# Real and imaginary rows packed in 96, logarithms summed in two parts, the sign from bits, and a new written-out order

## The chip, the cores and the metric

The kernel runs on one core of a Trainium2 chip. The metric is the device time of one execution in microseconds. Matrix products run on TensorE (PE in the profile, its weight loads PEld), elementwise work on VectorE (DVE) and ScalarE (ACT), a little on GpSimd (POOL); SyncE (SP) issues most DMAs.

## The reference

Two blocks follow each other. The first is a gated linear recurrence with a complex gate for each of 4 x 8 heads, 768 tokens and 48 channels; the second is a mixer over tokens of rank 32 and a two-layer network over 384 channels.

```python
mag = np.sqrt(a_re * a_re + a_im * a_im)
scale = np.minimum(mag, 0.999) / (mag + 1e-06)
a_re_n, a_im_n = (a_re * scale, a_im * scale)
for t in range(S):
    ar, ai = (a_re_n[:, :, t, :, None], a_im_n[:, :, t, :, None])
    new_re = ar * S_re - ai * S_im
    new_im = ar * S_im + ai * S_re
    kv = np.einsum('bhd,bhe->bhde', k[:, :, t], v[:, :, t])
    S_re, S_im = (new_re + kv, new_im)
    y[:, :, t] = np.einsum('bhd,bhde->bhe', q[:, :, t], S_re)
# x: the heads side by side, (4, 768, 384)
h = xt @ U @ V                      # xt: x with tokens last
u = x + h.transpose(0, 2, 1)
ch = np.maximum(u @ w_ch1, 0.0) @ w_ch2
out = u + ch
```

## The kernel before

Tokens are cut into 24 chunks of 128 (six for each of the four batches), two chunks to a group, so there are groups 0 to 11. The recurrence is not stepped: products of gates over a stretch of tokens are written as the exponential of a sum of logarithms of magnitudes and a turn by a sum of angles.

*Gates and totals* (`gates(g)`, rank "gates"): ScalarE and VectorE make from a_re and a_im the logarithm of the clipped magnitude, in two parts that stand in tiles `l` and `y` and are added on VectorE. TensorE sums the logarithm over tokens with constant matrices (`summed`: two sums for each chunk, line 696 for groups 0 to 2 in fp32, line 692 for the later groups, which split the logarithm in two fp32r tiles), and sums blocks of tokens (`of_blocks`: line 735 and line 741). ScalarE takes exponentials; the totals go by four DMAs into a tile T.

*Angles* (`turns_of`, `angles`, rank "angles"): an Arctan, a sign and a constant give the angle z (line 760), which is written over `y`; TensorE sums it over tokens; ScalarE takes sine and cosine into `cs`. The sign of a_re comes in groups 0 to 2 from its bits, by a VectorE operation that also puts 1/pi in (line 678), and in groups 3 to 11 from ScalarE's Sign; those groups then scale the angle and add a quarter in one more ScalarE operation. ScalarE works with two tables of functions in turn, so each group has two switches (line 381).

*Chunks* (`prep`, `chain`): q and k are multiplied by the exponentials and by sine and cosine into QKC, which holds for each head 48 real and 48 imaginary columns, each padded to 64. TensorE transposes QKC (line 860), from 64 tokens by 112 columns, to 112 partitions by 64 tokens, real rows at 0 and imaginary rows at 64. Products inside a chunk (lines 907, 910, 971), the state dk and its carrying on (line 996), and y (lines 1027, 1035) follow.

*Mixers* (`mixer(m)`): for each two chunks a product with w_ch1 (`up`, line 1122, or a scheme of fewer products, line 1222, in the last ones) and with w_ch2 (`down`, lines 1313 and 1356). The first mixer's six up-products are made before the mixing over tokens is known and are corrected later.

What runs when is written out by hand: each operation is added to a plan with its engine, a guessed cost and its rank, and ORDER gives, for each engine and rank, the place of each operation in one long list of 2671 places; each engine works through its operations in the order of their places. SPARE lists, for a place, how many blocks of 128 columns of idle matmul TensorE is given ahead of that operation. `idle` (line 1519) issues them, up to three blocks at a time, as a product of the identity with itself into a PSUM tile that is about to be used; where no such tile is free it issues nothing.

## Time and profile before

| | |
|---|---|
| three runs | 629.67, 630.09, 630.41 us; median 630.09 |
| profiled execution, span from the first to the last instruction | 627.0 us |
| its own time with what lies around the span | not given by itself; the median of the runs is 3.1 us above the span |
| TensorE busy, idle matmuls included | 609.9 us (97%) |
| VectorE busy | 499.7 us (80%) |
| ScalarE busy | 415.8 us (66%) |
| granted TensorE clock, mean | 0.995 |

A row of the groups names line, engine, operation, the tile written and those read, partitions by elements, and the count; then the busy time in us and the mean ns of one; then the engine's idle time just before, and what ended most of it. A row of the stretches gives the stretch and its length, the busy time and the number of instructions of PE, PEld, DVE, ACT and POOL (or of the engines chosen), then the granted clock, the share of DMA busy, and GB/s. A row of the waits gives who waited for whom, the sum, how often and the longest, in us. A row of the chain gives the start and the length of a piece in us.

### The profile page before, as it was taken

What the parts mean: (1) busy time and instruction counts of PE and PEld (TensorE: products, weight loads), DVE (VectorE), ACT (ScalarE), POOL (GpSimd) and SP (SyncE); (2) the same over time, 40 slices, a digit from 0 to 9 for tenths busy, and PEclk for the clock granted to TensorE, in tenths of its full rate; (3) what the DMA queues carried; (4) which work ended last, traced back from release to release, by engine and by line L of the source; (5) the groups of instructions that cost most, each with busy time, mean ns of one, the idle gap of its engine ahead of it and who ended that gap; (6) DMA issues with size and microseconds to landing.
All of it is one profiled execution on the core that took longest, in us unless ns stands there. A gap on an engine that the chain in (4) does not pass through costs nothing.

```text
span 627.0 us, 23447 instructions
## 1 busy us (share of the span) xinstructions
PE 609.9 (97%) x10380; PEld 526.2 (84%) x10380; DVE 499.7 (80%) x887; ACT 415.8 (66%) x807; POOL 38.1 (6%) x79
## 2 busy tenths in 40 slices
PE   6998989999999999999999999999999999999998
PEld 3566767666889889889989989888999998999997
DVE  6899999888999979758977867788989884464554
ACT  6999999999898988687787867688433431202010
POOL 5000000000001010010000100000100100000100
PEclk7999999999999999999999999999999999999999
DMA  8864565644143252541512512601203020000101
GB/s 211 191 146 115 135 136 132 155 111 104 33 80 76 50 120 44 99 89 28 99 37 46 113 40 46 124 19 25 63 21 60 9 51 3 1 1 1 45 14 44
DMA packets 173685, 45.74 MB, mean 73 GB/s; under 512 B 167632, under 2 KB 170384, under 8 KB 173584
## 3 DMA queue, kind: packets, MB, share of 16 engines
q1 hardware_dynamic: 171376, 39.90, 30.1%
q0 software_dynamic: 2208, 4.35, 2.1%
q8 instruction: 81, 1.33, 0.9%
q14 instruction: 20, 0.16, 0.1%
HBM read 33.59 MB, written 4.72 MB: 61 GB/s over the span
## 4 chain that ended last, share of the span: by engine, by line
PE 77%; ACT 4%; DVE 3%; DMA 1%; issue 1%; SPq 0%; ACTq 0%; DVEq 0%
PE down L1356 24%; PE up L1122 15%; PE few L1222 11%; PE dk L996 3%; PE tr L860 3%; PE y L1035 3%; PE inner L910 2%; PE down L1313 2%; PE inner L907 2%; PE tot L741 2%; PE y L1027 2%; PE mixed L1089 2%; PE es ps L692 1%; PE ef ps L692 1%; PE uTp L1107 1%; PE corners L971 1%
## 5 line engine op out<-in xcount | busy, mean ns | idle before, releaser
L1122 PE MATMUL up<-uT,w 128*128 128x256 f32 x504 | 116.9, 383 | 0.0
L387 DVE TENSOR_TENSOR QK<-QK,T 112x512 f32<-112x512 f32 (+2 forms) x144 | 102.1, 732 | 8.4 <-PE inner L910 4.3
L1122 PEld LDWEIGHTS up<-uT,w 128*128 128x128 f32 x504 | 93.6, 190 | 12.5
L1356 PE MATMUL down<-w,h 128*128 128x192 f32 x396 | 72.2, 331 | 0.0
L384 ACT ACTIVATE gate<-gate 128x768 f32<-128x768 f32 (+1 forms) x82 | 64.8, 795 | 7.4 <-DVE GS L791 3.2
L1356 PEld LDWEIGHTS down<-w,h 128*128 128x128 f32 x396 | 64.1, 190 | 1.5 <-issue 0.7
L871 ACT COPY QK<-tr 112x512 f32<-112x512 f32 x96 | 51.2, 590 | 14.6 <-PE tr L860 14.3
L390 DVE TENSOR_TENSOR xo<-down,xo 128x192 f32<-128x192 f32 (+1 forms) x79 | 29.9, 387 | 27.5 <-PE down L1356 27.0
L387 DVE TENSOR_TENSOR QKC<-qk,cs 128x768 f32<-128x768 f32 x44 | 41.7, 955 | 6.3 <-ACT cs L384 3.6
L1230 ACT COPY h<-few 128x512 f32<-128x512 f32 x30 | 17.2, 586 | 40.8 <-PE few L1222 40.8
L1356 PE MATMUL down<-stage 128*128 128x192 f32 x198 | 37.6, 331 | 0.0
L1111 ACT COPY uT<-uTp 128x384 f32<-128x384 f32 x22 | 10.0, 479 | 41.4 <-PE uTp L1107 26.9
L1222 PE MATMUL few<-gate,w 128*128 128x128 f32 x280 | 34.8, 275 | 0.0
L1298 POOL DMA_DIRECT2D out_dram<-xo x32 | 19.2, 644 | 243.3 <-DVE xo L390 140.0
L860 PEld LDWEIGHTS tr<-ident,QKC 64*112 64x112 f32 x768 | 24.5, 130 | 10.7 <-issue 4.7
L1222 PEld LDWEIGHTS few<-gate,w 128*128 128x128 f32 x280 | 33.3, 192 | 0.0
L1356 PEld LDWEIGHTS down<-stage 128*128 128x128 f32 x198 | 32.1, 190 | 0.7 <-issue 0.2
L779 POOL DMA_DIRECT2D gate<-F x15 | 12.0, 799 | 327.9 <-DVE w L578 113.5
L860 PE MATMUL tr<-ident,QKC 64*112 64x64 f32 x768 | 29.4, 221 | 2.3 <-DVE QKC L387 1.6
L381 ACT ACT_TABLE_LOAD x24 | 30.8, 1283 | 1.1 <-PEq L1573 0.7
L384 ACT ACTIVATE h<-up 128x512 f32<-128x512 f32 x42 | 24.6, 596 | 9.8 <-PE up L1122 9.5
L976 ACT COPY AT<-corners 32x128 f32<-32x128 f32 x96 | 24.2, 255 | 9.6 <-PE corners L971 8.3
(200 smaller groups left out, 1285.4 us busy)
## 6 DMA issues: line engine op xcount, KB each, us to landing
stage<-in_moe_w_ch_dram SPq DMA_DIRECT2D x12, 768.0 KB, 5.0
qk<-in_q_dram SPq DMA_DIRECT2D x24, 192.0 KB, 3.2
qk<-in_k_dram SPq DMA_DIRECT2D x24, 192.0 KB, 2.7
VP<-in_v_dram SPq DMA_DIRECT2D x24, 192.0 KB, 3.6
gate<-in_a_re_dram SPq DMA_DIRECT2D x22, 192.0 KB, 3.4
gate<-in_a_im_dram SPq DMA_DIRECT2D x22, 192.0 KB, 3.4
AT<-DG SPq DMA_DIRECT2D x96, 32.0 KB, 2.3
T<-E SPq DMA_DIRECT2D x48, 48.0 KB, 2.9
```

Source lines behind the costliest of these rows:

```text
L381: ACT(1.37, rank, lambda: nc.scalar.preload_act_table_set(name), writes=[TABLE])
L384: return nc.scalar.activation(out=o, in_=i, func=f, **kw)
L387: nc.vector.tensor_tensor(out=o, in0=a, in1=b, op=OP.mult)
L390: nc.vector.tensor_tensor(out=o, in0=a, in1=b, op=OP.add)
L860: nc.tensor.transpose(out=get(*ps[r])[0:DQ, h], in_=get(*qkc)[at, h].rearrange("p u d -> p (u d)")[:, 0:DQ], identity=ident[at, at], tile_ ...
L871: nc.scalar.copy(out=to, in_=a)
L976: ACT(0.36, RR, lambda r=r, u=u: nc.scalar.copy(out=get(*ATi).rearrange("p (a u) t -> p a u t", u=2)[r:r + BLK, :, u, BLK:2 * BLK], in_=ge ...
L996: nc.tensor.matmul(out=get(*dk[r])[x:end, h], lhsT=get(*ks)[at, h, x // DP, 0:end - x], rhs=get(*VPi)[at, h], start=True, stop=True, tile_ ...
L1122: nc.tensor.matmul(out=get(*ps)[:, e], lhsT=w1[:, f, (ff + e) * 128:(ff + e + 1) * 128], rhs=get(*uT)[:, f], start=(f == 0), stop=(f == KD ...
L1222: nc.tensor.matmul(out=get(*ps)[:, q], lhsT=w()[:, q * 128:(q + 1) * 128], rhs=v[0](), start=(n == 0 and q == 0), stop=True, skip_group_ch ...
L1298: queue.dma_start(out=out[b, c * CH:(c + 1) * CH, lo:hi], in_=get("xo", i)[:, lo:hi])
L1356: nc.tensor.matmul(out=get(*to)[:, part], lhsT=x(j), rhs=y[:, j], start=(first and j == 0), stop=(j == KH - 1), skip_group_check=not first)
```

## The change

QKC is packed: 96 columns for each head, real and imaginary side by side, with 32 columns of padding at the end of the tile. The transposed tiles, T and the state have 96 rows in place of 112. The second of the two state products takes 48 columns from column 64 of a head on, the last 16 of which belong to the next head and are not used. T is no longer filled with ones at the start.

In groups 0 to 2 the two parts of the logarithm are no longer added on VectorE; TensorE sums `y` and `l` one after the other into the same PSUM tile, in `summed` and in `of_blocks`. The clipping of `l` is on VectorE in these groups (before: group 0 alone; groups 1 and 2 had a Relu on ScalarE and a combined subtraction and addition on VectorE).

The sign comes from the bits in every group. The quarter is added where the angle is split in two (ScalarE in groups 4 to 11, VectorE in group 3, and VectorE for the second half).

ORDER is new in full, of 2658 places, and SPARE has 67 blocks in place of 153. The costs in the plan change with the operations above.

```diff
@@ in ORDER (the list is replaced as a whole; the lines that the prediction names)
-        ("PE", "mixing"): {0: [300, 462, 326, 490, 569, 509, 643, 645, 646, 688, 694, 722, 652, 653, 695, 696, 717, 736], 1: [783, 750, 789, 759, 824,
...
+        ('PE', 'mixing'): {0: [300, 423, 323, 468, 443, 502, 634, 635, 664, 678, 707, 719, 636, 677, 680, 681, 693, 712], 1: [773, 828, 833, 780, 756,
...
-        ("PE", "gates"): {0: [20, 32, 69], 1: [62, 63, 66], 2: [162, 163, 167, 168, 187, 188], 4: [331, 339, 343, 351, 352, 355], 6: [543, 525, 550,
-        545, 518, 514], 8: [669, 664, 674, 666, 678, 672], 10: [815, 816, 833, 836, 802, 804], 12: [1019, 1011, 1026, 1014, 1029, 1008], 14: [1192,
...
+        ('PE', 'gates'): {0: [30, 42, 66], 1: [49, 58, 64], 2: [165, 173, 163, 182, 191, 188], 4: [327, 343, 356, 365, 372, 369], 6: [497, 493, 522,
+        535, 538, 527], 8: [659, 652, 661, 671, 674, 646], 10: [800, 804, 820, 813, 795, 789], 12: [993, 985, 1008, 1019, 991, 984], 14: [1170, 1153,
...
-SPARE = {20: 8, 32: 9, 62: 1, 66: 1, 73: 1, 82: 5, 91: 1, 113: 6, 116: 1, 119: 8, 140: 8, 153: 6, 157: 4, 167: 1, 168: 1, 207: 6, 216: 1, 217: 1, 282:
-         1, 352: 2, 436: 1, 514: 5, 518: 5, 527: 4, 546: 4, 547: 25, 551: 12, 596: 2, 601: 1, 606: 3, 624: 1, 632: 3, 646: 1, 653: 1, 664: 1, 672: 2,
-         678: 5, 694: 1, 695: 1, 717: 1, 718: 2}
+SPARE = {30: 24, 76: 6, 95: 2, 101: 8, 119: 4, 146: 9, 152: 2, 215: 4, 248: 1, 268: 2, 275: 1, 567: 1, 603: 2, 624: 1}
...
@@ -265,8 +263,8 @@
 
     nc = tc.nc
     B, H, S, D = q.shape
+    DQ = 2 * D
     DP = 64
-    DQ = DP + D
     DM = H * D
     FF = moe_w_ch1.shape[1]
     R = moe_U.shape[1]
@@ -295,12 +293,12 @@
     TURN = 0.6
     EARLY, SPREAD = 2, (0,)
     SPLIT = range(3, NG)
+    SUMMED = range(SPLIT[0])
 
     TA, TC, TQ, TK, TF, TH, NTOT = 0, 8, 16, 20, 22, 30, 32
     NP = 128 // R
     PL = H * HC
 
-    BITS = range(SPLIT[0])
     PUT = (0, 2), (4, 6), (8, 10)
 
     AT_ONCE = (0, 1, 2)
@@ -456,8 +454,8 @@
     AT, DG, VP = [], [], []
     QKC = []
     for n in range(2):
-        QKC.append(singles.tile([128, H, 2, DP], FP, name="QKC%d" % n))
-        nc.gpsimd.memset(QKC[n][:, :, :, D:DP], 0.0)
+        QKC.append(singles.tile([128, H * DQ + DP - (DQ - DP)], FP, name="QKC%d" % n))
+        nc.gpsimd.memset(QKC[n][:, H * DQ:], 0.0)
     GATE = singles.tile([128, 6, GC * DM], FP, name="gate")
     AREA = {nm: GATE[:, n] for n, nm in enumerate(("x", "y", "n", "", "ar", "ai")) if nm}
     EF = [GATE[:, 3, n * DM:(n + 1) * DM] for n in range(GC)] + [singles.tile([128, DM], FP, name="ef%d" % n) for n in range(2)]
@@ -466,7 +464,6 @@
     TS = []
     for n in range(3):
         TS.append(singles.tile([DQ, GC, H * NTOT], FP, name="T%d" % n))
-        nc.gpsimd.memset(TS[n], 1.0)
     for n in range(3):
         VP.append(singles.tile([128, H, D], FP, name="VP%d" % n))
     for n in range(2):
@@ -654,10 +651,11 @@
             table(ca + 0.09, R1, lambda: act(t(y), t(l), AF.Exp, scale=-0.5, bias=leps), [L], Y)
             table(ca, R1, lambda: act(t(y), t(y), AF.Ln, bias=1.0), [], Y)
 
-            if on_dve:
+            if g in SUMMED or g in SPREAD:
                 DVE(c_one(W), R1, lambda: nc.vector.tensor_scalar(out=t(l), in0=t(l), scalar1=-0.5, scalar2=-LNMAX, op0=OP.mult,
                                                                   op1=OP.max), [], [L])
-                DVE(cd, R1, lambda: add(t(l), t(l), t(y)), Y, [L])
+                if g not in SUMMED:
+                    DVE(cd, R1, lambda: add(t(l), t(l), t(y)), Y, [L])
             else:
                 ACT(ca + 0.09, R1, lambda: act(t(l), t(l), AF.Relu, scale=-0.5, bias=lmax), [], [L])
                 DVE(cd, R1, lambda: nc.vector.scalar_tensor_tensor(out=t(l), in0=t(l), scalar=LNMAX, in1=t(y), op0=OP.subtract,
@@ -674,16 +672,13 @@
             table(ca, R1, lambda: act(t(x), t(x), AF.Ln), [], [X])
             table(ca, R1, lambda: act(t(x), t(x), AF.Exp, scale=-1.0), [], [X])
             DVE(cd, R1, lambda: mul(t(x), t(x), t(ai)), AI, [X])
-            if g in BITS:
-                DVE(c_one(W), R1, lambda: nc.vector.tensor_scalar(out=t(n).bitcast(U32), in0=t(ar).bitcast(U32), scalar1=0x80000000,
-                                                                  scalar2=INV_PI, op0=OP.bitwise_and, op1=OP.bitwise_or), AR, [N])
-            else:
-                ACT(ca + 0.09, R1, lambda: act(t(n), t(ar), AF.Sign, bias=tiny), AR, [N])
+            DVE(c_one(W), R1, lambda: nc.vector.tensor_scalar(out=t(n).bitcast(U32), in0=t(ar).bitcast(U32), scalar1=0x80000000,
+                                                              scalar2=INV_PI, op0=OP.bitwise_and, op1=OP.bitwise_or), AR, [N])
             for i in range(lo, hi):
                 within(i, R1, L)
 
         def within(i, R1, L):
-            ps, es = ("es ps", i), ("es", i)
+            ps, es, parts = ("es ps", i), ("es", i), (y, l) if g in SUMMED else (l,)
 
             def summed(m, name, to, keeps):
 
@@ -693,8 +688,10 @@
                 if g in SPLIT:
                     PE(0.35, R1, both, [("gs0", g), ("gs1", g), name], [to], takes=[keeps], steps=2)
                 else:
-                    PE(0.65, R1, lambda: nc.tensor.matmul(out=get(*to), lhsT=m.bitcast(FP), rhs=of(l, i), start=True, stop=True),
-                       [L, name], [to, ("sums", g, i)], takes=[keeps], steps=2)
+                    def each():
+                        for u, a in enumerate(parts):
+                            nc.tensor.matmul(out=get(*to), lhsT=m.bitcast(FP), rhs=of(a, i), start=(u == 0), stop=(u == len(parts) - 1))
+                    PE(0.65 * len(parts), R1, each, [L, name] + [y + (i,)] * (g in SUMMED), [to, ("sums", g, i)], takes=[keeps], steps=2 * len(parts))
             psum(ps, "T", [128, DM], [128, 512])
             if es not in APART:
                 buffer(es, "es", 2, [128, 2, DM])
@@ -732,8 +729,9 @@
                 for p in range(HH):
                     for u in range(2):
                         h, w = at + (u * HH + p) * D, 64 if u == 0 else D
-                        nc.tensor.matmul(out=get(*ps)[u * 64:u * 64 + w, p], lhsT=get(*l)[:, h:h + w], rhs=total, start=True,
-                                         stop=True, tile_position=(0, u * 64))
+                        for n, a in enumerate(parts):
+                            nc.tensor.matmul(out=get(*ps)[u * 64:u * 64 + w, p], lhsT=get(*a)[:, h:h + w], rhs=total, start=(n == 0),
+                                             stop=(n == len(parts) - 1), tile_position=(0, u * 64))
 
             def at_once():
                 for p in range(HH):
@@ -759,8 +758,6 @@
             table(ca, R2, lambda: act(t(x), t(x), AF.Arctan), [], [X])
             DVE(cd, R2, lambda: nc.vector.scalar_tensor_tensor(out=t(z), in0=t(x), scalar=math.pi / 4, in1=t(n),
                                                                op0=OP.subtract, op1=OP.mult), [X, N], Z)
-            if g not in BITS:
-                ACT(ca + 0.09, R2, lambda: act(t(z), t(z), AF.Identity, scale=1.0 / math.pi, bias=fourth), [], Z)
             if g in SPLIT:
                 for u in range(2):
                     ring(("zs%d" % u, g), "gs%d" % u, GS[u])
@@ -785,11 +782,12 @@
             if g in SPLIT:
                 a, b = ("zs0", g), ("zs1", g)
                 if g in MADE:
-                    ACT(c_act(DM), R2, lambda: nc.scalar.copy(out=of(a, i), in_=of(z, i)), [zi], [a + (i,)])
+                    ACT(c_act(DM) + 0.09, R2, lambda: act(of(a, i), of(z, i), AF.Identity, bias=fourth), [zi], [a + (i,)])
                 else:
-                    DVE(c_one(DM), R2, lambda: nc.vector.tensor_copy(out=of(a, i), in_=of(z, i)), [zi], [a + (i,)])
-                DVE(c_dve(DM), R2, lambda: nc.vector.tensor_tensor(out=of(b, i), in0=of(z, i), in1=of(a, i).bitcast(FP), op=OP.subtract),
-                    [zi, a + (i,)], [b + (i,)])
+                    DVE(c_one(DM), R2, lambda: nc.vector.tensor_scalar(out=of(a, i), in0=of(z, i), scalar1=0.25, scalar2=None, op0=OP.add),
+                        [zi], [a + (i,)])
+                DVE(c_dve(DM), R2, lambda: nc.vector.scalar_tensor_tensor(out=of(b, i), in0=of(z, i), scalar=0.25, in1=of(a, i).bitcast(FP),
+                                                                          op0=OP.add, op1=OP.subtract), [zi, a + (i,)], [b + (i,)])
 
                 def both():
                     for u in range(2):
@@ -834,6 +832,9 @@
 
 
 
+    def turns_of_heads(qkc):
+        return get(*qkc)[:, 0:H * DQ].rearrange("p (h u d) -> p h u d", u=2, d=D)
+
     def prep(i):
         R1 = "prep", i
         g = group_of(i)
@@ -857,7 +858,7 @@
                 for h in range(H):
                     for r in range(2):
                         at = slice(r * HC, (r + 1) * HC)
-                        nc.tensor.transpose(out=get(*ps[r])[0:DQ, h], in_=get(*qkc)[at, h].rearrange("p u d -> p (u d)")[:, 0:DQ],
+                        nc.tensor.transpose(out=get(*ps[r])[0:DQ, h], in_=get(*qkc)[at, h * DQ:(h + 1) * DQ],
                                             identity=ident[at, at], tile_position=(r * HC, 0))
             PE(TURN, R1, turn, [qkc], ps, way=5, takes=[QK], steps=2 * H)
 
@@ -986,14 +987,14 @@
             buffer(G, "G", 2, [DQ, H, D])
         parts_k = range(1 if last else 2)
         for r in parts_k:
-            psum(dk[r], "Y", [128, H, D], [128, H, DP])
+            psum(dk[r], "Y", [128, H, D], [128, H, HC])
 
         def state(h0):
             for h in range(h0, h0 + HH):
                 for r in parts_k:
                     at = slice(r * HC, (r + 1) * HC)
-                    for x, end in ((0, DP), (DP, DQ)):
-                        nc.tensor.matmul(out=get(*dk[r])[x:end, h], lhsT=get(*ks)[at, h, x // DP, 0:end - x], rhs=get(*VPi)[at, h],
+                    for x, w in ((0, DP), (DP, D)):
+                        nc.tensor.matmul(out=get(*dk[r])[x:x + w, h], lhsT=get(*ks)[at, h * DQ + x:h * DQ + x + w], rhs=get(*VPi)[at, h],
                                          start=True, stop=True, tile_position=(r * HC, x))
         for h0 in (0, HH):
             PE(0.5 if last else 0.497, RR, lambda h0=h0: state(h0), [ks, VPi], [dk[r] + (h0,) for r in parts_k], way=3,
...
```

53 lines of the change are left out of this document (27 added, 26 removed), and 242 rows, old and new, of the table ORDER.

## The prediction

> **What bounds the kernel now.** I read the stretches first, then TensorE's idle matmuls by stretch, then the waits of the early part, then groups for prices. The first view gives, for each stretch, its length and the busy time of TensorE, its weight loads, VectorE, ScalarE and GpSimd.
>
> ```profile
> span 627.0 us, 23447 instructions
> PE 609.9 (97%) x10380; PEld 526.2 (84%) x10380; DVE 499.7 (80%) x887; ACT 415.8 (66%) x807; POOL 38.1 (6%) x79
> 0.00:16.00 16.00, 10.79 (x21) 5.90 (x21) 10.50 (x28) 9.89 (x19) 8.41 (x32) 0.79 0.84 208
> 16.00:48.00 32.00, 30.37 (x534) 20.20 (x534) 30.38 (x52) 30.73 (x58) 0.00 (x0) 1.00 0.74 169
> 48.00:96.00 48.00, 43.31 (x1192) 32.48 (x1191) 47.83 (x75) 46.90 (x93) 0.00 (x0) 1.00 0.54 128
> 96.00:144.00 48.00, 45.86 (x618) 32.01 (x618) 42.05 (x65) 44.18 (x79) 0.96 (x1) 1.00 0.52 132
> 144.00:208.00 64.00, 64.00 (x1218) 54.53 (x1217) 60.97 (x98) 57.47 (x105) 4.19 (x6) 1.00 0.37 72
> 208.00:627.00 419.00, 415.58 (x6804) 381.06 (x6802) 307.96 (x573) 226.66 (x458) 24.50 (x40) 1.00 0.23 47
> ```
>
> There are two regimes. From 144 us TensorE is busy without a break, while VectorE is busy for 308 of the last 419 us and ScalarE for 227: nothing that shortens only those two engines there shortens the run. From 16 to 96 us it is the other way: VectorE is busy for 78.2 of 80 us and ScalarE for 77.6, so these two set the pace and TensorE waits for them. Its busy time hides how much it waits, since the kernel fills predicted gaps with idle matmuls on the identity matrix (line 1519), which count as busy. The same view of that line alone (TensorE's column first after the length):
>
> ```profile
> 0.00:16.00 16.00, 8.02 (x14) 4.37 (x14) 0.79 0.84 208
> 16.00:64.00 48.00, 14.79 (x50) 8.75 (x50) 1.00 0.65 149
> 64.00:112.00 48.00, 1.08 (x4) 0.68 (x4) 1.00 0.56 132
> 112.00:151.00 39.00, 6.71 (x24) 3.90 (x24) 1.00 0.59 145
> 151.00:627.00 476.00, 0.00 (x0) 0.00 (x0) 1.00 0.24 49
> ```
>
> So TensorE's waste has four parts. Before 96 us: 5.2 + 1.6 + 4.7 = 11.5 us idle and 8.0 + 14.8 + 1.1 = 23.9 us of idle matmuls. From 96 us on: 2.1 us idle to 144, 6.7 us of idle matmuls in 112 to 151, and 3.4 us idle after 208. Together 17.1 us idle (627.0 - 609.9) and 30.6 us of idle matmuls; the other 579.3 us are products that the result needs. A gain must come out of this waste, or out of the products themselves.
>
> What ends the early waits (waits of 0 to 144 us):
>
> ```profile
> PE es ps L696 <- DVE GL L390: 3.8, 1, 3.8
> PE tr L860 <- DVE QKC L387: 1.6, 4, 0.8
> PE inner L907 <- issue: 1.0, 1, 1.0
> ```
>
> The longest one, 3.8 us in the first stretch, ends with group 0's add of two logarithm parts, which the change removes. The others are mostly transposes that wait for VectorE. One wait of 1.0 us waits for nothing that the profile shows: the nearest thing to a late instruction packet.
>
> **The change part by part.** Products added. In groups 0 to 2 each sum of logarithms is made from two parts, so each of 12 sums has a second fp32 matmul of 384 columns, in two passes, and each of six chunks has its block totals twice. The rows for the price:
>
> ```profile
> 0.00:112.00 112.00, 10.88 (x24) 4.43 (x24) 0.97 0.64 150
> 0.00:112.00 112.00, 3.33 (x96) 3.02 (x96) 0.97 0.64 150
> 97.08 1.08 PE tr L860 x32
> 167.31 2.59 PE up L1122 x12
> ```
>
> The first two are the stretch view of lines 696 and 735, the others are from the chain. The added pass follows one on the same columns, so I price it by its streaming: 2.59 us for 12 passes of 256 columns is 0.843 ns a column, 0.324 us for 384, and 24 such passes are 7.8 us (the row's 10.9 us, with each group's start in it, is the upper bound). The totals double what they are now: between 1.9 us, if part of the 3.3 us is start, and 3.3; I take 2.4. Together 10.2 us of TensorE, all in the first 96 us. There they meet 35.4 us of waste, so I cost them at nothing: they run where an idle matmul or a gap is now. Without that cover they cost 10.2 us.
>
> VectorE and ScalarE in the saturated stretch. The prices:
>
> ```profile
> L390 DVE TENSOR_TENSOR GL<-GL,gate 128x384 f32<-128x384 f32 x2 | 1.1, 568 | 0.3 <-ACT gate L384 0.2
> L663 DVE SCALAR_TENSOR_TENSOR GL<-GL,gate 128x768 f32<-128x768 f32 x2 | 1.9, 954 | 0.0
> L678 DVE TENSOR_SCALAR gate<-gate 128x768 uint32<-128x768 uint32 x1 | 0.6, 559 | 0.0
> L384 ACT ACTIVATE GL<-GL,lmax 128x768 f32<-128x768 f32 x10 | 9.3, 930 | 0.1
> L384 ACT ACTIVATE gate<-gate,tiny 128x768 f32<-128x768 f32 x9 | 8.4, 938 | 0.0
> L384 ACT ACTIVATE gate<-gate,fourth 128x768 f32<-128x768 f32 x9 | 8.4, 931 | 2.3 <-DVE gate L760 2.1
> ```
>
> Group 0 loses two adds on VectorE (2 x 0.568). Groups 1 and 2 lose the Relu on ScalarE (2 x 0.930) and on VectorE trade the 0.954 us combination for a one-input operation priced by the sign row, 0.559. That is 1.9 us less for each engine, all before 96 us. As the two engines alternate, I take half as reaching the end: -0.9, with 0 and -1.9 as ends. Groups 3 to 11 lose the Sign and the shift by a quarter on ScalarE, 9 x (0.938 + 0.931) = 16.8 us, and give VectorE 9 x 0.559 = 5.0 us. Most of that lies after 144 us beside a TensorE that never stops, VectorE with 111 us free after 208: nothing on the path. If VectorE's slack between 144 and 208 us, 3.0 us, were used up, about two such operations (1.1 us) would show. The rewritten split of the angles keeps one operation for one operation; its bias on ScalarE costs less there than the shift just removed.
>
> One wait is added. In groups 0 to 2 the second logarithm part stays in y until the sums and totals have read it, and line 760 writes the angle over y. On VectorE the unpacking of weights and the next chunk's preparation are queued behind line 760, and the phase products wait for it. It was behind already: its input comes from an Arctan after the table switch, and that switch follows the exponentials of the same totals. I cost it at nothing; if a total came late, the chain behind it would pay that lateness as it does now.
>
> Packing in 96 rows. Work on 112 partitions becomes work on 96 with as many elements in each partition, so VectorE and ScalarE gain nothing. On TensorE most products keep their column counts and lose only contraction rows; weight loads of 64 and 112 rows take 134 and 137 ns, so I cost this at nothing. The transposes load 96 columns instead of 112:
>
> ```profile
> L1027 PEld LDWEIGHTS y<-VP,AT 64*64 64x64 f32 x768 | 14.0, 134 | 5.2 <-issue 2.3 <-ACT ef L384 0.6 <-ACT QK L871 0.5
> L1035 PEld LDWEIGHTS y<-GM,QK 112*64 112x64 f32 x384 | 13.2, 137 | 2.5 <-DVE QK L387 0.9 <-issue 0.5 <-DVE w L578 0.2
> L860 PEld LDWEIGHTS tr<-ident,QKC 64*112 64x112 f32 x768 | 24.5, 130 | 10.7 <-issue 4.7 <-DVE QKC L387 2.5 <-DVE F L807 1.0
> ```
>
> From the chain's row a transpose steps at 34 ns. If its columns set that, 768 x 34 x 16/112 = 3.7 us go; if the 64 streamed columns do, none. I take -1.0, nearer to none, because a load of 64x112 takes no longer than one of 64x64 here. [...]
>
> The order and its idle matmuls. The list SPARE falls from 153 blocks of 128 columns to 67. A block runs only if a PSUM tile is free, so I price by what ran: the 70 blocks listed up to position 282 ran by 64 us, in 8.0 + 14.8 = 22.8 us, 0.326 us each. The new list has 63 blocks up to position 275, about 20.5 us where 23.9 are now, but together with the added 10.2 that is 30.7 against 35.4 us of waste; it fits, and I take no gain from it. Later the old list has 83 blocks, of which 6.7 us ran between 112 and 151 us; the new one has four, 1.3 us. The order there brings needed work forward: of the first mixer's six up-products, number 4 moves from position 569 to 443 and the first products of group 3's sums from 514 to 493. So -5.4. Bounds: nothing, if idle time takes the place of the idle matmuls, and -6.7.
>
> The longer waits for packets that the search assumed can save no more than the 1.0 us wait above; I take 0. Twenty instructions fewer on ScalarE and seven more on VectorE, of 807 and 887, leave their packets nearly as they are; TensorE's grow by 120 of 10380. GpSimd loses three fills of T at the start and then waits for a load as before: 0.
>
> The sum: 627.0 - 5.4 - 0.9 - 1.0 = 619.7 us of span. The median of the runs, 630.09, is 3.1 above the profiled span; with the same 3.1 I get **622.8 us**.
>
> **The rivals.**
> 1. TensorE still waits after 112 us: idle time replaces the idle matmuls, since they stood where the searched order expected nothing to be ready. For it: VectorE (42.05) and ScalarE (44.18) are nearly full from 96 to 144 us. Against: the up-product moved forward. Then 627.0 - 0.9 - 1.0 = 625.1, or 628.2 us.
> 2. More comes out of the early waste. The start is re-ordered and the 3.8 us wait loses its add; if the 11.5 us idle before 96 us halves, another 5.7 us go: 614.0, or 617.1 us. Against it: both pacing engines are already at 97% from 16 us on.
> 3. Slower: the added products do not fit. TensorE becomes the bound before 96 us, because the 63 blocks still run whether a gap is there or not and the second product of a pair stands in the way of the chunk's transposes. It decides once idle matmuls and added products together pass the 35.4 us; at full price 619.7 + 10.2 = 629.9, or 633.0 us.
> 4. The clock. It is granted at 0.79 in the first 16 us and 1.00 in each later stretch. With fewer idle matmuls a long gap could bring the 0.79 back once: 0.21 x 16 = 3.4 us, 626.2 us. Against: the longest wait after the start is 1.0 us, so little needs covering. [...]
>
> **How the numbers follow.** Forecast 0.45; rival 1 0.20, rival 2 0.20, rival 3 0.12, rival 4 0.03. A measurement of this kernel can tell about 0.2% (1.3 us) from no change: 628.8 to 631.4 is the same. The forecast with its unknowns (transposes 0 to -3.7, relief 0 to -1.9, late blocks 0 to -6.7) lies almost wholly below, as do rivals 2 and 4; rival 1 at 628.2 puts about 0.06 into the same and 0.02 above; rival 3 is slower, with a little of the forecast's edge in the same. Faster 0.78, same 0.08, slower 0.14. The range takes in rivals 1, 2 and 4, goes 3 us under rival 2 for the transposes, and stops below rival 3: 614 to 631.
>
> **What would show it.** Right: line 1519 under 2 us after 112 us and TensorE still without idle there; line 696 with 48 matmuls before 112 us and TensorE's idle time before 96 us no larger than 11.5 us; transposes at 32 to 34 ns a step; ScalarE's total down by about 18 us, VectorE's up by about 3. Wrong: new waits of TensorE between 96 and 208 us (rival 1); TensorE full before 96 us while VectorE and ScalarE show gaps (rival 3); a granted clock under 1.00 after 16 us (rival 4).

## The result and the profile after

Nine executions of the changed kernel have a median of 632.30 us, nine of the kernel before 628.86 us: the ratio is 1.0049 (95% interval 1.0033 to 1.0066), so the change costs 0.5%, 3.4 us by the medians. The forecast was 622.8, faster. Of all executions behind the table further down one, of e_stage_late (638.55 us), fell in a slower state and is left out of its median and ratio. The profiled execution took 632.45 us with a span of 630.7, against a span of 627.0 before. Its totals and the stretches, with the same columns as before:

```profile
span 630.7 us, 23601 instructions
PE 616.1 (98%) x10464; PEld 530.5 (84%) x10464; DVE 501.2 (79%) x893; ACT 399.3 (63%) x787; POOL 35.2 (6%) x76
0.00:16.00 16.00, 13.91 (x74) 7.98 (x74) 10.07 (x28) 11.64 (x24) 5.36 (x29) 1.00 0.85 211
16.00:48.00 32.00, 30.95 (x581) 19.92 (x580) 31.57 (x55) 30.36 (x56) 0.00 (x0) 1.00 0.75 165
48.00:96.00 48.00, 43.27 (x946) 32.19 (x944) 40.84 (x64) 39.80 (x78) 0.00 (x0) 0.93 0.62 141
96.00:144.00 48.00, 45.90 (x860) 33.62 (x856) 43.68 (x70) 44.03 (x83) 0.96 (x1) 1.00 0.42 100
144.00:208.00 64.00, 64.00 (x1112) 53.31 (x1110) 60.35 (x96) 54.81 (x98) 4.80 (x7) 1.00 0.41 81
208.00:630.70 422.70, 418.08 (x6919) 383.46 (x6918) 314.66 (x585) 218.69 (x451) 24.08 (x39) 1.00 0.24 48
```

The idle matmuls alone (line 1520 now), and TensorE's time in the sums (line 693) and the totals (line 733) of groups 0 to 2:

```profile
0.00:16.00 16.00, 7.34 (x16) 3.90 (x16) 1.00 0.85 211
16.00:64.00 48.00, 10.78 (x34) 5.88 (x34) 0.99 0.71 163
64.00:112.00 48.00, 0.00 (x0) 0.00 (x0) 0.94 0.53 117
112.00:151.00 39.00, 1.68 (x6) 0.89 (x6) 1.00 0.49 115
0.00:112.00 112.00, 16.68 (x48) 8.71 (x48) 0.97 0.65 150
0.00:112.00 112.00, 6.17 (x192) 5.86 (x192) 0.97 0.65 150
```

The list did what it says. Idle matmuls fall from 30.6 to 19.8 us, idle time from 17.1 to 14.6 (630.7 - 616.1), so the waste shrinks by 13.3 us; the other products grow from 579.3 to 596.3. Products grew by 17.0 us and waste shrank by less, where the forecast had 9.2 (the added 10.2 less 1.0 for the transposes) against 16.5. Of the 17.0 us, 8.6 are the added sums and totals (16.68 - 10.88 and 6.17 - 3.33), 3.4 come from a lower clock (below), and some 5 are spread over the other products; no row says why those grew. The stretch that changed character is 48 to 96 us: VectorE and ScalarE, busy for 47.8 and 46.9 us before, now have gaps of 7 to 8 us each, and the clock is below 1.00 there.

What stands in that stretch, in order of time (start, length, line, operation, idle time before it and what ended it), and below it stretches of about 3.41 us laid where the granted clock changes:

```profile
58.87 0.93 PE L997 MATMUL dk<-VP,QKC 64*64 64x48 f32 x29
61.80 0.29 PE L997 MATMUL dk<-VP,QKC 64*64 64x48 f32 x3 [2.00 <-issue]
63.13 4.54 PE L1123 MATMUL up<-uT,w 128*128 128x256 f32 x12
68.24 1.16 PE L861 MATMUL tr<-ident,QKC 64*96 64x64 f32 x32
59.93:63.34 3.41, 1.54 (x39) 1.23 (x40) 2.69 (x7) 1.25 (x3) 0.00 (x0) 1.00 0.02 5
63.34:66.75 3.41, 3.41 (x9) 2.69 (x9) 1.82 (x2) 3.41 (x6) 0.00 (x0) 0.50 0.00 0
87.23:90.64 3.41, 1.46 (x46) 0.92 (x48) 2.07 (x3) 3.23 (x10) 0.00 (x0) 1.00 0.60 113
90.64:94.06 3.42, 3.42 (x40) 2.88 (x33) 3.35 (x6) 3.38 (x9) 0.00 (x0) 0.50 0.36 111
```

TensorE stops for 2.00 us in the middle of 32 like products, waiting for nothing that the profile shows; the clock is then 0.50 for one step of 3.41 us, and twelve up-products take 4.54 us instead of 2.6 to 2.9. A second gap, 2.11 us at 87.07, waits for VectorE, and another step at 0.50 follows. In the waits to 144 us the two are these:

```profile
PE ph L802 <- DVE F L805: 2.3, 2, 2.1
PE dk L997 <- issue: 2.0, 1, 2.0
```

At half clock for 3.41 us, each halved step costs 1.7 us of TensorE, 3.4 together.

### The profile page after: what moved, and what is told of

It reads as the page before. It is cut to its first block, busy times and chain, and to the rows that moved or that the text cites. A ratio compares the mean times of both kernels' runs of the same rounds, so it can differ in the third digit from the quotient of the medians.

```text
span 630.7 us, 23601 instructions
## 1 busy us (share of the span) xinstructions
PE 616.1 (98%) x10464; PEld 530.5 (84%) x10464; DVE 501.2 (79%) x893; ACT 399.3 (63%) x787; POOL 35.2 (6%) x76
## 3 DMA queue, kind: packets, MB, share of 16 engines
q8 instruction: 82, 1.34, 0.9%
## 4 chain that ended last, share of the span: by engine, by line
PE 80%; DVE 6%; ACT 5%; DMA 5%; SPq 3%; issue 2%; DVEq 0%; ACTq 0%
PE down L1357 22%; PE up L1123 17%; PE few L1223 11%; PE dk L997 3%; PE tr L861 3%; PE y L1036 3%; PE down L1314 3%; PE inner L911 2%; PE y L1028 2%; PE inner L908 2%; PE mixed L1090 2%; PE tot L739 1%; ACT gate L382 1%; DVE QK L385 1%; PE uTp L1108 1%
## 5 line engine op out<-in xcount | busy, mean ns | idle before, releaser
L1123 PE MATMUL up<-uT,w 128*128 128x256 f32 x504 | 118.7, 390 | 0.0
L385 DVE TENSOR_TENSOR QK<-QK,T 96x512 f32<-96x512 f32 (+2 forms) x144 | 102.4, 725 | 12.6 <-ACT QK L872 6.3
L1123 PEld LDWEIGHTS up<-uT,w 128*128 128x128 f32 x504 | 96.2, 194 | 13.8 <-ACT h L382 0.3
L872 ACT COPY QK<-tr 96x512 f32<-96x512 f32 x96 | 51.1, 583 | 14.3 <-PE tr L861 12.3
L861 PEld LDWEIGHTS tr<-ident,QKC 64*96 64x96 f32 x768 | 24.1, 123 | 9.1 <-issue 4.2
L997 PE MATMUL dk<-VP,QKC 64*48 64x48 f32 (+1 forms) x1408 | 28.6, 218 | 2.3 <-issue 2.0
L861 PE MATMUL tr<-ident,QKC 64*96 64x64 f32 x768 | 29.0, 220 | 1.5 <-DVE QKC L385 1.0
```

Of the source, the lines that this page charges most:

```text
L385: nc.vector.tensor_tensor(out=o, in0=a, in1=b, op=OP.mult)
L861: nc.tensor.transpose(out=get(*ps[r])[0:DQ, h], in_=get(*qkc)[at, h * DQ:(h + 1) * DQ], identity=ident[at, at], tile_position=(r * HC, 0))
L872: nc.scalar.copy(out=to, in_=a)
L997: nc.tensor.matmul(out=get(*dk[r])[x:x + w, h], lhsT=get(*ks)[at, h * DQ + x:h * DQ + x + w], rhs=get(*VPi)[at, h], start=True, stop=True, ...
L1123: nc.tensor.matmul(out=get(*ps)[:, e], lhsT=w1[:, f, (ff + e) * 128:(ff + e + 1) * 128], rhs=get(*uT)[:, f], start=(f == 0), stop=(f == KD ...
```

## The experiments

The changed kernel's profile lists a DMA queue of kind instruction with 82 packets, 1.34 MB together or 16 KB each; for which engine a packet is, it does not say. This profile left three theories. **Theory 1**: the 2.00 us stall is a wait for a late instruction packet; with the lower clock and the blocked SP queue behind it, it is the whole miss. **Theory 2**: the added products are not covered; they lie on the path (rival 3 of the prediction). **Theory 3**: the new order is worse by itself. Times are medians; ratios are against the kernel before on the same chip, with their intervals.

| kernel | what | us | ratio |
|---|---|---|---|
| e_split24 | changed, idle blocks issued singly up to 24 | 634.43 | 1.0102 (1.0064 to 1.0139) |
| e_split42 | changed, issued singly up to place 125 | 634.32 | 1.0076 (1.0047 to 1.0105) |
| e_vadd | changed, parts added on VectorE | 636.77 | 1.0118 (1.0087 to 1.0148) |
| e_vfill | the same with 24 more idle blocks | 636.39 | 1.0128 (1.0084 to 1.0172) |
| e_112 | changed, layout of 112 rows | 631.93 | 1.0041 (1.0015 to 1.0066) |
| e_stage_early | changed, one 768 KB load earlier | 634.04 | 1.0086 (1.0067 to 1.0104) |
| e_stage_small | changed, that load cut to 96 KB | 629.44 | 1.0018 (0.9997 to 1.0039) |
| e_stage_late | changed, that load later | 631.44 | 1.0059 (1.0029 to 1.0089) |
| e_noidle | changed, no idle matmuls | 643.35 | 1.0253 (1.0217 to 1.0289) |
| b_sum | before + sums on TensorE | 637.59 | 1.0140 (1.0127 to 1.0153) |
| b_sum_trim | the same, 31 idle blocks fewer | 637.40 | 1.0149 (1.0133 to 1.0165) |
| b_late | before, late idle blocks out | 629.67 | 1.0018 (1.0001 to 1.0035) |
| b_pack | before + packing | 627.72 | 0.9987 (0.9975 to 0.9999) |
| b_bits | before + sign from bits, quarter in the split | 629.46 | 1.0021 (1.0011 to 1.0032) |
| b_rest | before + both of these | 630.78 | 1.0036 (1.0022 to 1.0049) |

**Moving the packet boundaries.**

```diff
-            idle(min(run, AHEAD))
-            run -= min(run, AHEAD)
+            k = min(run, 1 if at < 40 else AHEAD)      # e_split42: at < 125
+            idle(k)
+            run -= k
```

> The changed kernel, with the idle matmuls of the first 24 listed blocks issued one block of 128 columns at a time instead of several blocks in one instruction: the same idle columns, 64 more instructions on TensorE, so that every later product of TensorE sits at another place in its instruction packets. Theory 1 (the 2.00 us stall at 59.8 us is a late instruction packet; with the lower clock behind it and the SP queue blocked, it costs 7 to 8 us): the stall at 59.8 us goes or moves, the clock stays at 1.00 there, and the time falls to 624 to 627, if no other packet comes late. Theory 2 (the added products of 10.1 us are on the path): 631 to 633, as the changed kernel, wherever the packet boundaries fall.

> As the kernel before it in this list, with all idle blocks up to 125 issued singly, some 108 more instructions on TensorE: another shift of the packet boundaries. Theory 1: a time between 624 and 634 that goes with whether a stall on a packet of over 1.5 us stands in the first 100 us: with none, 624 to 627; with one, 631 to 634. Theory 2: 631 to 633, stall or none.

Neither came near 624 to 627. In e_split24 the stall near 60 us is still there, longer (2.94 us at 59.73, now before other products), and more such waits stand elsewhere; in e_split42 there are three of 1.25 to 1.45 us before 90 us. A stall that keeps its time while the instructions move under it does not come from where a packet ends alone. Theory 1 needed a cause tied to the time.

**Sums off TensorE, and the old layout, in the new order.**

```diff
+                    add(t(l), t(l), t(y))        # e_vadd: in the clipping's step; sums and totals single again
-    DQ = 2 * D
+    DQ = DP + D                                  # e_112
```

> The changed kernel, with the two logarithm parts of groups 0 to 2 added on VectorE, in the same step of the order, so that TensorE multiplies the sums and totals once, as before the change; the rest of the order stands. TensorE loses 10.1 us of products before 96 us, VectorE gains 2.7 us. Theory 2: the time falls by most of the 10 us less VectorE's 2.7, to 623 to 626. Theory 1: about 160 TensorE instructions fewer shift the packets, so the stall at 59.8 us may go: 624 to 627 without a stall, 629 to 632 with one. The rival to both, that the order itself is worse: 630 to 633.

> The changed kernel with the layout of 112 rows put back (real rows, padding, imaginary rows), all else as changed, with the same instructions on TensorE. Transposes of 112 columns: between 0 and 2.7 us more by the bounds of the prediction; the comparison of the two traces (transposes 0.2 us shorter) says nothing that can be measured: 631 to 633, with the same stall at 59.8 us by theory 1.

All theories had e_vadd at 633 or below; it is slower than the changed kernel. Without the second products TensorE waits more often between 10 and 92 us, once for 2.99 us on issue, and the mean granted clock is 0.987. Three of the clippings, now joined with the add, also stand 3.5 to 7.5 places later, so that the second part is there. Later the gaps were filled with idle blocks:

```diff
-SPARE = {30: 24, 76: 6, 95: 2, 101: 8, 119: 4, 146: 9, 152: 2, 215: 4, ...
+SPARE = {30: 24, 76: 6, 95: 2, 101: 8, 119: 4, 146: 9, 152: 4, 215: 4, ... 64: 4, 169: 3, 416: 3, 548: 3, ...
```

> The changed kernel with the log parts added on VectorE, as in the run with single sums before, and 24 idle blocks of 128 columns listed where that run's TensorE waited for data (positions 64 to 548), some 8 us. Theory: the new order without the added products is the better one, and only the clock, granted at 0.987 there, took it away. Then the clock is at 0.995 or more in most executions and the time 623 to 628, faster than both kernels. If the blocks push products back: 630 to 634. If the stall on a packet near 61 us stays with the lower clock behind it, 3 us more than without.

636.39, and 632.34 and 632.36 in its two executions with a mean clock of 0.997 or more. So even at nearly full clock the new order without the sums is no better than with them. Why is not shown: the order was laid around the second products, and the later clippings stand in these runs too, as does, in e_vfill's profile, a stall on issue of 2.46 us. Both runs are misses, and they say that the parts of this change do not simply add up.

e_112 is not to be told from the changed kernel (1.0041 against 1.0049). Its trace holds the cleanest sight of the clock: the same stall, 2.07 us, and no halved step.

```profile
62.03 0.29 PE L998 MATMUL dk<-VP,QKC 64*64 64x48 f32 x3 [2.07 <-issue]
63.37 2.86 PE L1124 MATMUL up<-uT,w 128*128 128x256 f32 x12
66.78 1.16 PE L862 MATMUL tr<-ident,QKC 64*112 64x64 f32 x32
57.47:60.88 3.41, 2.48 (x121) 2.11 (x117) 3.14 (x5) 2.23 (x4) 0.00 (x0) 1.00 0.67 210
60.88:64.30 3.42, 2.27 (x42) 1.88 (x43) 2.34 (x5) 1.46 (x3) 0.00 (x0) 1.00 0.02 5
84.78:88.19 3.41, 1.79 (x13) 0.59 (x13) 1.70 (x4) 3.23 (x8) 0.00 (x0) 1.00 0.53 103
```

The clock's steps lie elsewhere in this execution (its one drop in the record, at 627.5 us, after the last instruction, gives their place, counted back in 3.41 us); the gap is shared between two of them, TensorE is busy for 2.48 and 2.27 us of them, and the up-products take 2.86 us. Its span is 626.9; of the 3.8 us between this execution and the changed kernel's profile, the two halved steps can account for 3.4. Of its twelve executions the four with a mean clock of 0.996 or more took 628.68 to 631.25 us, the four with 0.991 took 632.76 to 636.15. In 96 executions of the kernel before, taken beside the runs of the table, no such slope is to be seen (43 at 1.00 average 628.8, 34 at 0.997 628.5, 13 at 0.995 629.6, five at 0.991 or 0.992 629.0): in its profile the clock is 0.50 from 8.10 to 14.92 us alone, largely on idle matmuls (4.05 of TensorE's 6.12 busy us there). The changed kernel's nine executions have 0.992 to 0.997, none 1.00; that is too narrow for a slope of their own. Transposes of 96 and of 112 columns take the same 1.16 us for 32, here and above, though a weight load of theirs is 7 ns shorter in the changed kernel (123 ns, where 130 stood before):

```profile
L861 PEld LDWEIGHTS tr<-ident,QKC 64*96 64x96 f32 x768 | 24.1, 123 | 9.1 <-issue 4.2 <-DVE QKC L385 1.9 <-DVE F L805 0.7
```

**What the late packet waits for.** The DMA records in the traces back the name: a 16 KB instruction packet lands at 60.54 us in the changed kernel, at 60.73 in e_112 and at 59.53 in e_stage_small, and the stall ends 1.3 to 1.4 us later in each; in the kernel before one lands at 95.29 us, and its 1.05 us wait on issue ends at 96.84, 1.55 us later. The burst ahead of the stall is a 768 KB load of staged weights.

```diff
-6.6: [284]            # place of the load on SP
+6.6: [274.5]          # e_stage_early
+            few = slice(0, 16 if p == 6 else 128)      # e_stage_small: 16 of 128 partitions
+6.6: [320.5]          # e_stage_late, and the operations that read it:
-        ('ACT', 'w1'): 6: [310, 333]    ('DVE', 'w1'): 6: [320, 348, 403]
+        ('ACT', 'w1'): 6: [363.5, 366.5]    ('DVE', 'w1'): 6: [370.5, 380.5, 409.5]
```

> The changed kernel, with one 768 KB load of staged weights (load 6.6) issued by SP two places earlier, ahead of a load that waits: at about 52 us instead of 54.91. Theory 1, made narrower by the first runs: the instruction packet at 59.44 us came late because it stood behind this load's data in the DMA engines (busy share 0.89 to 0.90 from 56 to 60 us). Then the burst ends some 2 us earlier, the stall at 59.8 us shrinks from 2.00 to under 1 us, the clock stays at 1.00 behind it, SP is free again some 3 us earlier, and the time is 624 to 628. Theory 2 (the added products are on the path): 630 to 633, whatever the stall does.

> The changed kernel, with the same load cut to 16 of its 128 partitions (96 KB instead of 768 KB): the weights of one half are left as they were for the others, so the mixer's result of that half is not the reference's; all instructions stay. Theory 1: no burst from 56 to 60 us, no stall on a packet at 59.8 us, clock 1.00 there, and SP's loads for group 3 issued by 70 to 76 us, so the second wait of 2.11 us at 87 us goes too: 623 to 627. Theory 2: 630 to 633. If the stall stays though the burst is gone, the packet is late for another reason than the data ahead of it.

> The changed kernel with the 768 KB load behind the late instruction packet (load 6.6) moved past SP's wait near 68 us, and the five operations on ScalarE and VectorE that read it moved later to match; nothing is left out. Theory 1 (the packet is late because of the data ahead of it; cutting the load to 96 KB brought the stall from 2.00 to 0.70 us and the span to 626.1): no burst from 56 to 60 us, stall under 0.8 us, clock 1.00 behind it, 626 to 629.5 in most executions. If the five moved operations hold others up, TensorE waits for weights or data between 80 and 110 us instead, and it is 630 to 633.

The stretches 56 to 58 and 58 to 60 us of the changed kernel, of e_stage_small and of e_stage_late (the last columns are the clock, the share of DMA engines busy, GB/s):

```profile
56.00:58.00 2.00, 2.00 (x66) 1.82 (x64) 2.00 (x4) 1.89 (x4) 0.00 (x0) 1.00 0.90 240
58.00:60.00 2.00, 1.78 (x98) 1.42 (x93) 2.00 (x4) 1.79 (x4) 0.00 (x0) 1.00 0.89 260
```
```profile
56.00:58.00 2.00, 1.70 (x54) 1.53 (x54) 1.93 (x4) 1.61 (x3) 0.00 (x0) 1.00 0.56 131
58.00:60.00 2.00, 1.99 (x112) 1.75 (x109) 1.81 (x3) 1.34 (x4) 0.00 (x0) 1.00 0.24 49
```
```profile
58.00:60.00 2.00, 1.99 (x103) 1.75 (x99) 1.64 (x3) 1.00 (x4) 0.00 (x0) 1.00 0.04 8
```

With DMA 0.89 busy the stall is 2.00 us, with 0.24 it is 0.70, with 0.04 there is none, so in these three the stall goes with the load ahead of it. So far the stall is what theory 1 says, its price is not. e_stage_small is 2.9 us under the changed kernel by the medians but still not faster than before. e_stage_late removes the stall without leaving work out and gains nothing that can be told from the changed kernel: in its profile TensorE waits 1.7 us for ScalarE from 76.8 us on, ahead of a total, and two halved steps follow (0.50 from 80.45 to 87.28 us). In e_stage_early the stall is gone too, but a transfer of 32 KB comes 1.1 us late behind the moved load, with two halved steps behind it (0.50 from 57.70 to 64.53 us). In both a wait near by took the place of the one removed, and the clock came down behind it.

**The sums alone, in the old order.**

```diff
+    SUMMED = range(SPLIT[0])
-                        nc.tensor.matmul(... rhs=of(l, i), start=True, stop=True)
+                        for u, a in enumerate(parts):   # (y, l); the totals likewise
+                            nc.tensor.matmul(... rhs=of(a, i), start=(u == 0), stop=(u == len(parts) - 1))
```

> The kernel before, with one part of the change alone: the two parts of the logarithm of groups 0 to 2 are summed on TensorE (sums and totals twice), VectorE's two adds and ScalarE's two Relu go, and the order and idle matmuls are those of before. The prediction's step (added products of 10.1 us meet early waste): idle matmuls of before stay listed, but the gaps shrink, so 0 to +3 us against before, 629 to 632. Theory 2 (they do not fit): most of the 10.1 us shows, 635 to 640. Theory 1 adds: some 100 TensorE instructions more before 96 us, so a stall on a packet may come anywhere, +2 to +4 each with the clock.

637.59 us, +8.9 by the medians, theory 2's range. The profiled execution ran at clock 1.00 throughout, with a span of 636.2, 9.2 more than before, and no matmul waits on issue for more than 1.0 us before 112 us: neither clock nor late packets are needed for it. Its stretches, the totals of all and of the idle matmuls, and the sums and totals of groups 0 to 2:

```profile
16.00:48.00 32.00, 30.63 (x505) 20.22 (x504) 25.80 (x44) 26.56 (x48) 0.00 (x0) 1.00 0.71 161
48.00:96.00 48.00, 44.53 (x1103) 32.92 (x1099) 43.59 (x72) 42.44 (x87) 0.00 (x0) 1.00 0.46 104
sum 636.20, PE 619.75 PEld 533.36 DVE 498.24 ACT 415.36 POOL 37.85; mean PE 123.95 PEld 106.67 DVE 99.65 ACT 83.07 POOL 7.57
sum 636.20, PE 30.05 PEld 17.43; mean PE 7.51 PEld 4.36
0.00:112.00 112.00, 18.45 (x48) 9.14 (x48) 1.00 0.61 143
0.00:112.00 112.00, 6.16 (x192) 5.82 (x192) 1.00 0.61 143
```

The added products cost 10.4 us there (18.45 - 10.88 and 6.16 - 3.33). The idle matmuls take 30.05 us, as before (30.6), and idle time is 16.45 (636.20 - 619.75) where it was 17.1. The waste hardly moved, and the added time went on top. VectorE and ScalarE, busy for 78.2 and 77.6 of these 80 us before, are busy for 69.4 and 69.0, of which some 1.9 us each, by the prediction's rows, is work taken away: they wait now, and for what, the waits to 112 us say, before and in b_sum:

```profile
ACT gate L384 <- PE ef ps L696: 2.0, 1, 2.0
ACT E L384 <- PE tot L741: 0.7, 1, 0.7
ACT E L384 <- PE tot L735: 0.6, 2, 0.4
ACT es L384 <- PE es ps L692: 0.5, 1, 0.5
```
```profile
ACT gate L389 <- PE ef ps L702: 3.1, 4, 1.5
ACT E L389 <- PE tot L742: 3.1, 5, 0.8
ACT es L389 <- PE es ps L702: 1.2, 2, 1.0
ACT h L389 <- PE es ps L702: 0.9, 2, 0.6
ACT ef L389 <- PE ef ps L702: 0.7, 2, 0.4
```

ScalarE waits 9.0 us on sums and totals where it waited 3.8, and VectorE's angle (line 760 before, 768 here) waits 3.5 us for ScalarE where it waited 0.3: the lateness that the prediction named and costed at nothing. The second products stand between the logarithm and its exponential, on the chain of the engines that set the pace; TensorE's spare time lies at other moments. This is the old order. In the changed kernel's own profile one row of such waits is left before 112 us:

```profile
ACT E L382 <- PE tot L733: 1.1, 3, 0.6
```

There ScalarE hardly waits on sums and totals; the new order has moved that wait away, and this mechanism is not to be seen in it.

The counter-test takes out as much idle matmul time as the second products need:

```diff
-SPARE = {..., 32: 9, ..., 113: 6, ..., 119: 8, 140: 8, ..., 207: 6, ...
+SPARE = {..., ..., 113: 2, ..., 119: 2, 140: 2, ..., ...
```

> The kernel before with the sums and totals of groups 0 to 2 made from two parts on TensorE, in the old order (637.6 us), and 31 of its 153 idle blocks taken out ahead of and between those products (31 x 0.326 = 10.1 us, the price of the added products). The prediction's step (the products run where an idle matmul is now): 628 to 631. If the idle matmuls stood in gaps that VectorE and ScalarE set, so that taking them out only turns them into idle time: 634 to 638.

```profile
sum 636.30, PE 614.72 PEld 530.02 DVE 498.47 ACT 416.17 POOL 37.56; mean PE 122.94 PEld 106.00 DVE 99.69 ACT 83.23 POOL 7.51
sum 636.30, PE 22.00 PEld 13.27; mean PE 5.50 PEld 3.32
```

Idle matmuls fell by 8.05 us, idle time rose by 5.1 to 21.6, the other products show 3.0 us more (why, no row says), and the time stayed (637.40). These idle matmuls stood in gaps that others set. They were no reserve.

**Idle matmuls otherwise.**

```diff
-SPARE = {30: 24, 76: 6, ...}
+SPARE = {}                       # e_noidle, in the changed kernel
-SPARE = {..., 514: 5, 518: 5, 527: 4, ... 718: 2}
+SPARE = {..., 436: 1}            # b_late, in the kernel before
```

> The changed kernel without its idle matmuls (19.8 us of TensorE). If they stand in the way of products (the prediction's third rival): faster by some us, 625 to 629. If they only fill gaps and keep the clock up: the granted clock falls below 1.00 in more stretches before 64 us than the changed kernel's, and the time is 633 to 640. If they do neither: 630 to 633.

> The kernel before without the 80 idle blocks listed from position 514 on, of which 6.7 us ran between 112 and 151 us; nothing else. The prediction's step for the late blocks (5.4 us gained where the old order stands): 622 to 625. Its first rival (idle time takes their place): 627 to 630, with TensorE idle 5 to 7 us more between 112 and 151 us. If the clock falls in the gaps: 630 to 634.

Without any, the changed kernel takes 643.35 us. Its profiled execution, the longest of six with 650.16 us, has a clock of 0.79 and 0.86 where there was 1.00 and 0.93:

```profile
16.00:48.00 32.00, 24.66 (x475) 16.99 (x473) 27.43 (x48) 27.82 (x50) 0.00 (x0) 0.79 0.67 149
48.00:96.00 48.00, 41.33 (x954) 30.90 (x951) 38.35 (x61) 38.02 (x73) 0.00 (x0) 0.86 0.56 124
```

So here they fill gaps and hold the clock. b_late tests the largest gain forecast in the old order: 112 to 151 us, before and in b_late:

```profile
112.00:151.00 39.00, 37.70 (x281) 23.43 (x281) 33.85 (x48) 36.53 (x61) 1.74 (x2) 1.00 0.59 145
112.00:151.00 39.00, 36.04 (x268) 20.64 (x268) 34.33 (x49) 37.43 (x61) 1.82 (x3) 1.00 0.58 144
```

The 6.7 us of idle matmuls are gone, TensorE is idle 1.7 us more, and the other 5 us are taken by its other products, of which 268 instead of 257 fall in the stretch; how much of that is hidden waiting is not shown. No time is saved: 629.67 us.

**Packing and sign.** 

> The kernel before, in its own order and with its own idle matmuls, with the rest of the change without the sums: rows packed in 96, the sign from bits and the quarter inside the split for groups 3 to 11 (ScalarE some 17 us less, VectorE some 5 us more). The prediction's steps cost these at nothing to -1.0 us: 627.5 to 629.5. If the sums are all that costs (theory 2), the same. Rival: VectorE's nine added operations come before 208 us often enough to show: 630 to 632.

> The kernel before with the packing in 96 rows alone. The prediction's step: transposes 0 to 3.7 us shorter, 1.0 taken: 625 to 629. From the runs so far (transposes 0.2 to 0.3 us shorter at 96 columns): 628 to 629.5. If the packing carries the 2 us of the run with both: 630 to 632.

> The kernel before with the sign from bits and the quarter inside the split for groups 3 to 11 alone (ScalarE some 17 us less, VectorE some 5 us more). The prediction's step: nothing on the path, 628 to 629.5. If VectorE's nine added operations are what cost the 2 us of the run with both: 630 to 632.

Their edits are the parts of the printed diff for QKC, T and dk (b_pack), and for the sign and the split with the freed places deleted and VectorE's operation put where ScalarE's Sign stood (b_bits). Packing gains 0.1%, with an interval that just leaves out no change; as one of fifteen comparisons that is weak. The sign costs 0.2%. Together they cost 0.4%, which the two singles do not add up to; that stays open. In b_bits's profile the wait on issue that stood at 95.79 us before is 2.05 us long instead of 1.05, with one halved step behind it (0.52 from 98.00 to 101.50 us), and that accounts for 2.7 us of a single execution; whether it makes the median is not shown.

## Why the prediction was wrong

**The step that failed first** is "they meet 35.4 us of waste, so I cost them at nothing". The price of the products was right: 10.2 us by sum, 10.4 us in b_sum. The cover was wrong: in the old order 9.2 us of it came out in the span. The 35.4 us was added up over stretches as if TensorE could use any of it at any time; b_sum_trim shows that it can't. How much of the cost is left in the new order, no run separates. Rival 3 named the mechanism (the second product of a pair stands in the way) and the time, 633.0, but set its condition at the sum of 35.4 us and so gave it 0.12. That 632.3 lies near its time is luck: 633.0 still counts the 5.4 us of the late idle matmuls as gained. Its sign came by half: VectorE and ScalarE show gaps, but TensorE is not full, idle for 4.7 us between 48 and 96 us. The condition in place of the sum is who waits for the product: ScalarE did already, 3.8 us before 112 us.

**The late idle matmuls, -5.4.** They went as said (6.7 to 1.68 us between 112 and 151), but b_late puts their worth in the old order at nothing. That comes near rival 1, with 0.20. In the changed kernel TensorE's idle time in that stretch rose only from 1.3 to 2.1 us, and still no time was saved.

**The clock.** Rival 4's price, 3.4 us, is what two halved steps cost; its chance, 0.03, leaned on the longest wait being 1.0 us, in a profile whose order and loads the change replaced. "Issue" waits costed at nothing became one of 2.00 us behind a 768 KB load. e_stage_small, with most of that load left out and 0.70 us of stall remaining, is 2.9 us faster by the medians; the whole miss is 9.5. The profile before has 0.50 once, for two steps from 8.10 us on; the step ahead of them has 0.32 us of work and lies in the wait of 3.8 us:

```profile
4.69:8.10 3.41, 0.32 (x2) 0.00 (x0) 1.96 (x5) 2.65 (x6) 2.67 (x10) 1.00 0.99 297
8.10:11.51 3.41, 2.71 (x5) 1.53 (x6) 2.90 (x6) 2.98 (x7) 3.07 (x12) 0.50 0.87 172
```

In the changed kernel's profile the clock fell behind gaps of 2.00 and 2.11 us, in steps with 1.54 and 1.46 us of work.

**The smaller terms.** Transposes -1.0: packing gains 0.6 us by the medians, so the size was near by luck: 32 transposes take the same time as before (1.16 us, 1.15 at 97.01 us in the profile before), so not for the reason given. The other end of that term, 3.7 if the columns set the step, is not borne out either: a load of 96 columns takes 123 ns, one of 112 took 130. VectorE and ScalarE gain next to nothing from 96 rows, as said: VectorE's product of QK with T takes 681 ns on 96x512 and 687 on 112x512, ScalarE's copy into QK 583 and 590. The bias in the split adds 95 ns to an operation of ScalarE (612 for 517), twice a group, where the shift took 931 once. Relief -0.9: its part in the three groups is inside b_sum's net 8.9; the sign in the later groups, costed at nothing, costs 0.2%.

**What was right.** 48 matmuls on the sums' line before 112 us, idle matmuls under 2 us after 112 us, ScalarE's total down by 16.5 us and VectorE's up by 1.5, idle time before 96 us at 7.9 us (2.1 + 1.05 + 4.73), under the 11.5. One half of a sign failed, TensorE's idle time after 112 us (2.1 us to 151). The rest could come true without a gain, since none of it measured the chain.

**The ledger.** Sums +8.9 us and packing with sign +2.2 in the old order make 11.1; the change came to +3.4. By that subtraction the new order with its shorter list gives some 7.7 us back, part of which the clock takes again. It is a subtraction only: e_vadd shows that order and sums do not run apart cleanly. Theory 1 is at most a part of the miss; theory 2 is shown in the old order; theory 3 stays open, for the subtraction speaks against it, and e_vfill, at 632.3 us with nearly full clock where the kernel before has 628.6, speaks for it. Of all kernels here only packing alone comes out below the kernel before: 627.72 us, 0.9987 (0.9975 to 0.9999).

## What to carry to other kernels

Idle matmuls and idle time on an engine are no reserve until a run has shown that something can use them: ask of each added product who reads it next and whether that reader was already waiting. Where two engines set the pace, price a product that stands between them at its full length on their chain. A new order needs a fresh look at what each large load is put ahead of, instruction packets among them, and at gaps of 2 us on TensorE: a halved step behind one cost 1.7 us more.

## What the hardware showed unexpectedly

In these profiles the granted clock changes in steps of 3.41 us: 0.50 from 63.34 to 66.75 and from 90.64 to 94.06 us in the changed kernel, and once more from 629.95 us, just before its end; from 8.10 to 14.92, two steps, in the kernel before. The steps lie at other places from one execution to the next (57.70 us begins one in e_stage_early, 80.45 in e_stage_late). A stall of 2.00 us had a halved step behind it in the changed kernel's profile (span 630.7), one of 2.07 us in e_112's had none (626.9). Busy time in a step does not decide alone: steps with 1.46 and 1.54 us of work were followed by half clock, and so were one with 1.91 in e_stage_late and one with 2.10 in e_stage_early, while one with 1.79 in e_112, placed as above, was not.

Waits on issue stop TensorE for up to 2.99 us in these runs (e_vadd). In the three runs that differ by one load they go with the data in flight: 2.00, 0.70 and 0 us with the DMA engines 0.89, 0.24 and 0.04 busy from 58 to 60 us. That share does not set the length alone: b_bits stalls for 2.05 us from 94.82 us on, behind these two stretches:

```profile
91.00:93.00 2.00, 2.00 (x10) 1.77 (x10) 2.00 (x5) 1.99 (x4) 0.00 (x0) 1.00 0.93 300
93.00:95.00 2.00, 1.82 (x91) 1.32 (x90) 2.00 (x3) 1.97 (x4) 0.00 (x0) 1.00 0.28 108
```

Most instruction packets cost the matmuls no wait that the profile lists: beside the 82 of the changed kernel stand two waits of matmuls on issue, of 2.0 and 0.5 us.
